# A two-stage convolution and gated projection: the first convolution of all columns on TensorE in small overlapping superblocks, products of two blocks grouped by shape of the array

## The chip, the cores and the metric

The kernel runs on one core of one Trainium2 chip. A core has TensorE (matrix products, in the profile PE, and PEld for its weight loads), VectorE (DVE), ScalarE (ACT), GpSimd (POOL) and SyncE (SP, which here issues DMAs). The metric is the device time of one execution in microseconds; lower is better. Three runs of the kernel before took 463.28, 458.24 and 459.96 us, so the time before is the median, 459.96 us.

## The reference, cut to what matters

```python
# x: (8, 4224, 192), weight: (8, 7), conv_w: (5, 192), w_val and w_out: (192, 192)
w = softmax(weight, axis=-1)                       # one set of 7 taps per head of 24 channels
x_pad = concatenate([zeros(6 rows), x])            # causal
x = einsum('hk,bskhg->bshg', w, x_unf)             # first convolution, per head
gate_pre = 0
for k in range(5):                                 # second convolution, per channel, causal
    gate_pre += conv_w[k] * xp[:, k:k + S, :]
gate = 1 / (1 + exp(-gate_pre))
out = (gate * (x @ w_val)) @ w_out
```

`moe_w_val`, `moe_conv_w` and `moe_w_out` arrive as float64, and their bits are put together to float32 on the chip (`decode`).

## The kernel before, in words

**Layout.** The eight sequences are laid end to end, with zero rows between, in two streams of four sequences each. Channels lie on partitions and time on columns: channels 0 to 127 of the streams side by side in one tile (`x1`, two halves), channels 128 to 191 of both streams stacked in one tile of 128 partitions (`x2`: 64 rows for each stream).

**First convolution.** Columns come in groups (`NJS`, `TOKS`). The first group, 456 columns, is convolved element by element (`conv_first`, L264: ACT, DVE and POOL). All others go through TensorE: a window of 128 rows of x in time (122 new ones and 6 of overlap), 120 channel-and-run columns wide, is the stationary operand; a banded matrix of the softmaxed taps (`band`, one per head, written by SP's DMAs at L170) is the moving one, 122 columns. One window is one float32 matmul, which the trace shows as two instructions. A bank holds up to four windows (`conv_unit`, L309); ACT copies it to a tile `e` (L331). The rows of `e` are then moved to `x1` and `x2` by DMA on SP's queue: for groups 1 and 2 through DRAM (`bounce`, written at L352, gathered at L294 and L298), for the others straight, from five runs of rows to five stretches of columns (`conv_scatter`, L342, issue at L385). The 4 columns of history of a group are copied from the group before by POOL (`conv_edges`, L247).

**Blocks.** Columns are worked in 36 blocks (`STEPS`), mostly of 488. For a block n: `gate_open` (ACT, L407) and four `gate_taps` (DVE, L414) for each of two accumulators in PSUM make the second convolution; `gate_close` is the sigmoid (ACT, L427). `split1` and `split2` write x as a high and a low part of reduced float32 (ACT, then POOL, L435 to L444). The product with `w_val` takes three matmuls for each pair of parts. `product1` (L452) makes channels 0 to 127: for each stream three matmuls with 128 rows (L457 to L459), then three pairs with 64 rows, one in each half of the array's rows (L464). `product2` (L467) makes channels 128 to 191: three matmuls with 128 output columns, half of them zero weights (stream 1), three with 64 output columns (stream 0), both L472, and three with a block-diagonal weight for `x2` (L475). `gated` multiplies with the gate (DVE, L504); the result is split again and goes through the same two products with `w_out`; `project` copies (ACT, L519) and stores. The last block's `w_out` product is made in float32 (`product_whole`, L478).

**Order.** PE, ACT, DVE and POOL run in the order written out at L585 to L609. In turn n: the `w_val` products of block n, taps and split of block n + 1, the `w_out` products of block n - 1, and convolution banks in four places, as many as `due` asks for. 44 convolution units are issued ahead of the loop (L576 and L580). PSUM has eight banks: two for convolution, two and one for the gate's accumulators, three for products.

Of the kernel before, what the change touches and what calls it, by code (L numbers as in the profile page):

```python
# [7 lines left out]
F32 = mybir.dt.float32  # L8
# [4 lines left out]
ALU = mybir.AluOpType  # L13
PSUM = bass.MemoryType.PSUM

# [5 lines left out]
NS = 5  # L21
PADB = S + KW - 1 + KG - 1
SEQS = 4


NP = 456
NJS = [0, 4, 8, 8, 8, 8, 8, 8, 2]
NG = len(NJS)
TOKS = [n * NS * WIN // 2 if n else NP for n in NJS]
STREAM = sum(TOKS)  # L30
EV = [t + t % 2 for t in TOKS]
XC = max(EV) + HALO
RUNM = max(NJS) * WIN

BOUNCED = (1, 2)
XBUFS, EBUFS = 4, 3

LOADS = (0, 1, "x2", "wv", 2, 3, "x3", 4, 5, "wo", 6, 7)


CB = 2
C0 = 28

BLOCKS = {456: (456,), 610: (306, 304), 1220: (408, 406, 406), 2440: (488,) * 5}
MB = 488
STEPS = []
for _g, _t in enumerate(EV):
    _o = 0
    for _n in BLOCKS[_t]:
        STEPS.append((_g, _o, _n))  # L50
        _o += _n

LAST = len(STEPS) - 1


@with_exitstack
def kernel(
# [3 lines left out]
    xc: bass.AP,  # L63
# [15 lines left out]
    dp = ctx.enter_context(tc.tile_pool(name="dp", bufs=1, space=bass.MemoryType.DRAM))  # L79
# [6 lines left out]
    w0 = cp.tile([128, 2, KW], F32, name="w0")  # L86
    nc.sync.dma_start(w0, hw)
    scr = [op.tile([128, 3 * MB], F32, tag="ot", name=f"scr_{i}") for i in range(3)]
# [11 lines left out]

    xpre = gp.tile([128, 2, MB], F32, tag="g1", name="xpre")
    xpre2 = gp.tile([128, MB], F32, tag="g2", name="xpre2")
    NX = NP + KW - 1

    heads = [(g, h) for g in range(1, NG) for h in range(NH)]
    xtiles, xoff, loaded = {}, {}, [0]
    o = 0
    for g, h in heads:
        xoff[g, h] = o
        o += WK * NJS[g] * NS * HC  # L110

    def load_x(i):

        if i != loaded[0] or i == len(heads):
            return
        loaded[0] += 1
        g, h = heads[i]
        n = NJS[g] * NS * HC
        t = xin.tile([WK, max(NJS) * NS * HC], F32, tag="x", name=f"x_{g}_{h}")
        o = xoff[g, h]  # L120
        nc.sync.dma_start(t[:, :n], xw[o : o + WK * n].rearrange("(p f) -> p f", f=n))
        xtiles[g, h] = t

# [3 lines left out]
    with tc.manual_schedule(engines={mybir.EngineType.SP}):  # L127
        nc.sync.dma_start(xpre[:, :, :NX], xc[:, :2, :])
        nc.sync.dma_start(xpre2[:, :NX], xc[:, 2, :])
        load_x(0)  # L130
        load_raw("cw")
        load_x(1)

        one = cp.tile([128, 1], F32, name="one")
        nc.vector.memset(one, 1.0)
        warm = cp.tile([128, 1], F32, name="warm")
        nc.scalar.activation(warm, one, AF.Exp)
        rrow = 2 * WIN + KW

        row = cp.tile([128, 2, rrow], F32, name="row")  # L140
        nc.gpsimd.memset(row, 0.0)

        def wide(t):
            return t[:, :, None].to_broadcast([128, 2, KW])

        mx = cp.tile([128, 2], F32, name="mx")
        nc.vector.tensor_reduce(out=mx, in_=w0, op=ALU.max, axis=mybir.AxisListType.X)
        w1 = cp.tile([128, 2, KW], F32, name="w1")
        nc.vector.tensor_tensor(out=w1, in0=w0, in1=wide(mx), op=ALU.subtract)
        w2 = cp.tile([128, 2, KW], F32, name="w2")  # L150
        nc.scalar.activation(w2, w1, AF.Exp)
        warm2 = cp.tile([128, 1], F32, name="warm2")
        nc.scalar.activation(warm2, w2[:, 0, 0:1], AF.Sigmoid)
        sm = cp.tile([128, 2], F32, name="sm")
        nc.vector.tensor_reduce(out=sm, in_=w2, op=ALU.add, axis=mybir.AxisListType.X)
        sm2 = cp.tile([128, 2], F32, name="sm2")
        nc.vector.tensor_scalar(out=sm2, in0=sm, scalar1=1e-9, scalar2=None, op0=ALU.add)
        rs = cp.tile([128, 2], F32, name="rs")
        nc.vector.reciprocal(rs, sm2)
        taps = row[:, :, WIN - 1 : WIN - 1 + KW]  # L160
        nc.vector.tensor_tensor(out=taps, in0=w2, in1=wide(rs), op=ALU.mult)


        band = cp.tile([WK, NH, WIN], F32, name="band")

        def load_band(h):
            c, p = divmod(h * HC, 128)
            r = row[p : p + 1, c, :]
            src = bass.AP(tensor=r.tensor, offset=r.offset, ap=[list(r.ap[0]), [1, WK], [1, WIN]])
            nc.sync.dma_start(band[:, h, :], src)  # L170

        for k in LOADS:
            if k in raw:
                load_raw(k)
            elif k in ("x2", "x3"):
                load_x(int(k[1]))
            else:
                load_band(k)
# [31 lines left out]
    pr = decode("cw", 2 * KG)  # L210
    put(cwt.rearrange("p a k -> p (a k)"), pr, 0, 128, 0, 2 * KG)

    W11, W21, WZ, W12, W22 = 0, 128, 256, 320, 384
    NW = 512

    class Weight:
        def __init__(self, name):  # L220
            self.name = name
            self.f = cp.tile([128, NW], F32, name=f"{name}f")
            self.h = cp.tile([128, NW], F32R, name=f"{name}h")
            self.l = cp.tile([128, NW], F32R, name=f"{name}l")
            nc.gpsimd.memset(self.f, 0.0)

        def make(self):
# [7 lines left out]
            nc.scalar.copy(self.h, t)  # L235
            nc.vector.tensor_tensor(out=self.l, in0=t, in1=self.h.bitcast(F32), op=ALU.subtract)
# [3 lines left out]
    x1s, x2s = {}, {}  # L240

    def conv_open(g):
        x1 = xp.tile([128, 2 * XC], F32, tag="x1", name=f"x1_{g}")
        x2 = xp.tile([128, XC], F32, tag="x2", name=f"x2_{g}")
        x1s[g], x2s[g] = x1, x2

    def conv_edges(g):  # L247

        x1, x2 = x1s[g], x2s[g]
        x1v = x1.rearrange("p (a t) -> p a t", a=2)  # L250
        if g == 0:
            nc.gpsimd.memset(x1v[:, :, 0:HALO], 0.0)
            nc.gpsimd.memset(x2[:, 0:HALO], 0.0)
        else:
            t = TOKS[g - 1]
            p1 = x1s[g - 1].rearrange("p (a t) -> p a t", a=2)
            nc.gpsimd.tensor_copy(x1v[:, :, 0:HALO], p1[:, :, t : t + HALO])
            nc.gpsimd.tensor_copy(x2[:, 0:HALO], x2s[g - 1][:, t : t + HALO])
        if EV[g] > TOKS[g]:
            t = HALO + TOKS[g]  # L260
            nc.gpsimd.memset(x1v[:, :, t : t + 1], 0.0)
            nc.gpsimd.memset(x2[:, t : t + 1], 0.0)

    def conv_first():  # L264

        conv_open(0)
# [412 lines left out]
```

## Time and profile before

| | us |
|---|---|
| median of three runs | 459.96 |
| the profiled execution, span from first to last instruction | 457.0 |
| TensorE busy | 416.4 |
| VectorE busy | 358.4 |
| ScalarE busy | 327.1 |
| GpSimd busy | 255.1 |

The span lies 3.0 us under the median of the runs. Durations of single instructions on PE, DVE and ACT overlap with the next one's, so a cost per instruction is read from start to start. In a timeline row stand the start, the length, the engine, the line, the operation, the tiles (written<-read), the shape (for a matmul rows*columns of the weights, then the moving operand), the count, and in brackets what the engine waited for. In a table by stretch stand, after the times, the busy time of PE, PEld, DVE, ACT and POOL, the granted clock of TensorE (1.00 is full), the share of the DMA engines and GB/s.

### The profile page before, as it was taken

The numbers are of one execution on the slowest core, as the hardware profiler recorded it, in microseconds if no ns is written. First come the engines' busy times: TensorE is split into PE (matmuls) and PEld (weight loads), VectorE is DVE, ScalarE is ACT, GpSimd is POOL, SyncE is SP. The second block draws the span as 40 slices with busy tenths as digits, with TensorE's granted clock in tenths as the row PEclk, the third lists the DMA queues.
The fourth block names the chain that finished last, engine by engine and source line by source line (L and its number), as shares of the span: only waits on it lengthen the run. The fifth ranks groups of instructions, "written<-read, shape, count | busy, mean of one in ns | idle before, by whom it ended". The sixth has DMA issues, their size and how long they took to land.

```text
span 457.0 us, 7190 instructions
## 1 busy us (share of the span) xinstructions
PE 416.4 (91%) x2371; PEld 321.7 (70%) x2371; DVE 358.4 (78%) x449; ACT 327.1 (72%) x537; POOL 255.1 (56%) x173
## 2 busy tenths in 40 slices
PE   2379659579999999999999999999999999999997
PEld 2268548467777777777777777777777777776773
DVE  5993983346998887888878888788887889999960
ACT  7335356275887777778777777777877788888852
POOL 5900522252776665566655666556665567768750
PEclk9657999969999999999999999999999999999999
DMA  7765855588878987666676766657666553322322
GB/s 199 172 207 186 287 187 195 192 271 199 245 184 255 276 221 225 178 218 207 180 215 183 221 212 174 213 169 224 216 184 200 143 154 101 108 84 89 135 115 99
DMA packets 30989, 85.95 MB, mean 188 GB/s; under 512 B 7272, under 2 KB 14504, under 8 KB 30952
## 3 DMA queue, kind: packets, MB, share of 16 engines
q1 hardware_dynamic: 30952, 85.50, 61.7%
q8 instruction: 18, 0.29, 0.3%
q14 instruction: 19, 0.16, 0.1%
HBM read 33.68 MB, written 31.62 MB: 143 GB/s over the span
## 4 chain that ended last, share of the span: by engine, by line
PE 75%; DMA 18%; ACT 3%; POOL 2%; issue 1%; SPq 0%; ACTq 0%
PE pc L324 15%; DMA bounce<-e 12%; PE pv L472 10%; PE po L472 9%; PE po L464 6%; PE pv L464 6%; PE po L475 5%; PE pv L475 4%; DMA x<-bounce 4%; PE po L457 3%; PE po L459 3%; PE pv L457 3%; PE po L458 3%; PE pv L459 3%; PE pv L458 3%; POOL x L280 2%
## 5 line engine op out<-in xcount | busy, mean ns | idle before, releaser
L414 DVE SCALAR_TENSOR_TENSOR pa<-x,cwt,pa 128x976 f32<-128x976 f32 (+5 forms) x144 | 172.5, 1198 | 18.9 <-ACT pa L407 16.5
L324 PE MATMUL pc<-band,x 128*120 128x122 f32 x864 | 123.4, 290 | 26.6 <-ACT e L331 18.2
L324 PEld LDWEIGHTS pc<-band,x 128*120 128x120 f32 x864 | 113.2, 198 | 45.4 <-ACT e L331 22.2
L436 POOL TENSOR_TENSOR pl<-g,ph 128x976 fp32r<-128x976 f32 (+4 forms) x35 | 78.3, 2236 | 89.8 <-ACT ph L435 85.1
L436 POOL TENSOR_TENSOR xl<-x,xh 128x976 fp32r<-128x976 f32 (+5 forms) x36 | 79.1, 2198 | 82.1 <-ACT xh L435 80.3
L331 ACT COPY e<-pc 120x488 f32<-120x488 f32 (+2 forms) x128 | 63.0, 502 | 74.1 <-PE pc L324 40.6
L504 DVE TENSOR_TENSOR g<-pv,g 128x488 f32<-128x488 f32 (+5 forms) x108 | 66.4, 642 | 52.1 <-ACT pb L407 23.8
L414 DVE SCALAR_TENSOR_TENSOR pb<-x,cwt,pb 128x488 f32<-128x488 f32 (+5 forms) x144 | 102.2, 710 | 3.7
L519 ACT COPY ot<-po 128x488 f32<-128x488 f32 (+5 forms) x108 | 56.0, 553 | 25.1 <-PE po L464 16.2
L444 POOL TENSOR_TENSOR pl<-g,ph 128x488 fp32r<-128x488 f32 (+4 forms) x35 | 42.6, 1217 | 8.0 <-ACT ph L443 8.0
L407 ACT ACTIVATE pa<-x,cwt 128x976 f32<-128x976 f32 (+5 forms) x36 | 37.8, 1051 | 11.7 <-DMA x<-bounce 10.4
L444 POOL TENSOR_TENSOR xl<-x,xh 128x488 fp32r<-128x488 f32 (+5 forms) x36 | 43.1, 1197 | 0.0
L472 PE MATMUL pv<-xh,wvh 128*128 128x488 f32 (+5 forms) x72 | 31.1, 432 | 8.4 <-ACT ot L519 7.6
L427 ACT ACTIVATE g<-pa 128x976 f32<-128x976 f32 (+5 forms) x36 | 34.6, 962 | 5.3 <-DVE pa L414 4.7
L435 ACT CAST xh<-x 128x976 fp32r<-128x976 f32 (+5 forms) x36 | 34.7, 964 | 4.5 <-DMA x<-bounce 2.4
L435 ACT CAST ph<-g 128x976 fp32r<-128x976 f32 (+4 forms) x35 | 34.4, 984 | 0.0
L457 PE MATMUL pv<-xh,wvh 128*128 128x488 f32 (+5 forms) x72 | 29.8, 416 | 2.2 <-DVE g L504 2.2
L472 PE MATMUL po<-ph,woh 128*128 128x488 f32 (+4 forms) x70 | 30.2, 431 | 0.0
L457 PE MATMUL po<-ph,woh 128*128 128x488 f32 (+4 forms) x70 | 29.0, 415 | 0.0
L472 PE MATMUL pv<-xl,wvh 128*128 128x488 f32 (+5 forms) x72 | 27.4, 381 | 0.0
L472 PE MATMUL pv<-xh,wvl 128*128 128x488 f32 (+5 forms) x72 | 27.4, 381 | 0.0
L459 PE MATMUL pv<-xl,wvh 128*128 128x488 f32 (+5 forms) x72 | 27.2, 378 | 0.0
(92 smaller groups left out, 688.9 us busy)
## 6 DMA issues: line engine op xcount, KB each, us to landing
x<-xw SPq DMA_DIRECT2D x48, 480.0 KB
out<-ot SPq DMA_DIRECT2D x30, 732.0 KB
x<-e SPq DMA_DIRECT2D x165, 91.5 KB
bounce<-e SPq DMA_DIRECT2D x8, 457.5 KB
x<-bounce SPq DMA_DIRECT2D x1, 1952.0 KB
x<-xw SPq DMA_DIRECT2D x8, 240.0 KB
bounce<-e SPq DMA_DIRECT2D x8, 228.8 KB
x<-bounce SPq DMA_DIRECT2D x3, 488.0 KB
```

Source lines behind the costliest of these rows:

```text
L324: nc.tensor.matmul(pc[: NS * HC, j * WIN : (j + 1) * WIN], lhsT=xtiles[g, h][:, jj * NS * HC : (jj + 1) * NS * HC], rhs=band[:, h, :], sta ...
L331: nc.scalar.copy(e[: NS * HC, q * hr : (q + 1) * hr], pc[: NS * HC, :hr])
L414: nc.vector.scalar_tensor_tensor(out=acc, in0=views(n, k)[i], scalar=cwt[:, i, k : k + 1], in1=acc, op0=ALU.mult, op1=ALU.add,)
L435: nc.scalar.copy(h, x)
L436: nc.gpsimd.tensor_tensor(out=l, in0=x, in1=h.bitcast(F32), op=ALU.subtract)
L444: nc.gpsimd.tensor_tensor(out=l, in0=x, in1=h.bitcast(F32), op=ALU.subtract)
L457: nc.tensor.matmul(acc, lhsT=w.h[:, r], rhs=h[:, q], start=True, stop=False)
L459: nc.tensor.matmul(acc, lhsT=w.h[:, r], rhs=l[:, q], start=False, stop=False)
L464: nc.tensor.matmul(acc, lhsT=a[p, r], rhs=b[p], start=False, stop=(i == 2))
L472: nc.tensor.matmul(o, lhsT=a[:, r], rhs=b[:, q], start=(q == 1 and i == 0), stop=False)
L504: nc.vector.tensor_tensor(out=v, in0=pvs.pop((n, q)), in1=v, op=ALU.mult)
L519: nc.scalar.copy(ots[n][:, q * m : (q + 1) * m], acc)
```

## The change

All columns are convolved on TensorE. They come in 13 superblocks of n = 1, 2, 4 and then ten times 5 windows for each of five runs, which give 286, 606, 1216 and 1506 columns (the last 1264). Superblocks overlap by the history they need: no columns are copied from the one before, and some windows are made twice (456 windows over all heads in place of 432). The rows of `e` are now in channel-major order and the channels are permuted (`PERM`), so one DMA moves a whole head where it took several: 13 for a superblock. The DRAM tile goes. The band's eight DMAs are issued by ACT.

Blocks are mostly 502 wide; there are again 36. In each, channels 128 to 191 of both streams are made by float32 matmuls of 64 output columns (`columns`), four quarters of the block for two halves of the array's columns, in place of six matmuls on split parts. Products of block n with `w_val` and of block n - 1 with `w_out` are put together by their shape: the diagonal ones, the full ones, the column ones, the row ones. The last block takes the same way as the others. Convolution banks and products share one PSUM pool of five banks. The gate's tiles `g1`, `g2` have two buffers in place of three, `x1`, `x2` three in place of two. The convolution of superblock g is spread over the blocks of superblock g - 2; superblocks 0 and 1 are convolved ahead of the loop. SP's order is written out too.

```diff
-NJS = [0, 4, 8, 8, 8, 8, 8, 8, 2]
+NJS = [1, 2, 4] + [5] * 10
+BLOCKS = {1: (286,), 2: (304, 302), 4: (406, 406, 404), 5: (502, 502, 502)}
+QUADS = ((6, 7, 5, 0), (1, 2, 3, 4))
+PER_LOAD = {1: 4, 2: 2, 4: 1, 5: 1}
+XBUFS, EBUFS = 6, 3
+LAG = 2
...
-    xp = ctx.enter_context(tc.tile_pool(name="xp", bufs=2))
+    xp = ctx.enter_context(tc.tile_pool(name="xp", bufs=3))
...
-    gp = ctx.enter_context(tc.tile_pool(name="gp", bufs=3))
+    gp = ctx.enter_context(tc.tile_pool(name="gp", bufs=2))
...
-    ps_c = ctx.enter_context(tc.tile_pool(name="ps_c", bufs=2, space=PSUM))
...
-    ps_v = ctx.enter_context(tc.tile_pool(name="ps_v", bufs=3, space=PSUM))
+    ps = ctx.enter_context(tc.tile_pool(name="ps", bufs=5, space=PSUM))
...
+    for q in QUADS:
+        for h in q:
...
-            nc.sync.dma_start(band[:, h, :], src)
+            nc.scalar.dma_start(band[:, h, :], src)
...
+        def send(dst, c0, c1, a, b):
+            w = NS * (b - a)
+            dma(dst[:, :w].rearrange("p (s t) -> p s t", s=NS), rows(c0, c1)[:, a:b])
+
+        if h < 5:
+            send(x1[h:120:5], 0, HC, 0, r)
+        else:
+            ends = (0, hf), (r - hf, r)
+            if h == 5:
+                for i, (a, b) in enumerate(ends):
+                    send(x1[120:128, i * second(n) :], 0, 8, a, b)
+            for i, (a, b) in enumerate(ends):
+                if h == 5:
+                    send(x2[64 * i + 48 : 64 * i + 64], 8, HC, a, b)
+                else:
+                    send(x2[64 * i + h - 6 : 64 * i + 48 : 2], 0, HC, a, b)
...
+    def diagonal(what, n):
...
+        r = slice(W22, W22 + 128)
+        for i, (a, b) in enumerate(parts(w, h2, l2)):
+            nc.tensor.matmul(acc, lhsT=a[:, r], rhs=b, start=(i == 0), stop=False)
...
+    def columns(what, n):
...
+        m = STEPS[n][2]
+        acc = banks[what, n, 2]
+        w = w_val if what == "v" else w_out
+        x = views(n)[0] if what == "v" else g1s[n]
+        cuts = [m * i // 4 for i in range(5)]
+        for i in range(4):
+            c = slice(cuts[i], cuts[i + 1])
+            for q, p in enumerate(HALVES):
+                nc.tensor.matmul(
+                    acc[p, c], lhsT=w.f[:, W12 : W12 + 64], rhs=x[:, q, c],
+                    start=False, stop=(i == 3),
+                )
...
+    conv(first_unit[1])
+    w_val.make()
+    load_raw("wo")
+    gate_open(0, 0)
+    gate_open(0, 1)
+    gate_taps(0, 0)
+    gate_taps(0, 1)
+    split(0)
+    gate_close(0, 0)
+    gate_close(0, 1)
+    conv(first_unit[LAG] - done[0])
+    w_out.make()
+    gate_open(1, 0)
+    gate_open(1, 1)
+
+    for n in range(N + 1):
+        todo = max(0, (due[n] if n < N else 0) - done[0])
+        c = [todo // 4 + (i < todo % 4) for i in (3, 0, 2, 1)]
+        diagonal("v", n)
+        gate_taps(n + 1, 0, 1, 3)
+        split(n + 1)
+        diagonal("o", n - 1)
+        main("v", n, 0)
+        conv(c[0])
+        main("v", n, 1)
+        gate_taps(n + 1, 0, 3, KG)
+        columns("v", n)
+        gated(n, 2)
+        gate_close(n + 1, 0)
+        gate_open(n + 2, 0)
+        columns("o", n - 1)
+        split_gated2(n)
+        project(n - 1, 2)
+        rows("v", n)
+        gated(n, 0)
+        gated(n, 1)
+        rows("o", n - 1)
+        split_gated1(n)
+        main("o", n - 1, 0)
+        gate_taps(n + 1, 1)
+        project(n - 1, 0)
+        conv(c[1])
+        main("o", n - 1, 1)
+        conv(c[2])
+        project(n - 1, 1)
+        conv(c[3])
+        gate_close(n + 1, 1)
+        gate_open(n + 2, 1)
```

`main` makes the three full matmuls of one stream (as L457 to L459 before), `rows` the three pairs in the array's two row halves (as L464 before).

More of the change, by code (lines that the diff above doesn't have):

```diff
@@ new lines @@
+    load_x(2)
+    load_raw("cw")
+    load_raw("wv")
+    load_x(4)
+    one = cp.tile([128, 1], F32, name="one")
+    nc.vector.memset(one, 1.0)
+    warm = cp.tile([128, 1], F32, name="warm")
+    nc.scalar.activation(warm, one, AF.Exp)
+    rrow = 2 * WIN + KW
+    row = cp.tile([NH, rrow], F32, name="row")
+    nc.gpsimd.memset(row, 0.0)
+    mx = cp.tile([NH, 1], F32, name="mx")
+    nc.vector.tensor_reduce(out=mx, in_=w0, op=ALU.max, axis=mybir.AxisListType.X)
+    w1 = cp.tile([NH, KW], F32, name="w1")
@@ L247, in conv_edges @@
[L247 to L262, printed above, removed]
@@ L307 @@
[L307 to L323 removed]
+    x1s, x2s, es = {}, {}, {}
@@ L387 @@
-    N = len(STEPS)
-    first = [next(n for n in range(N) if STEPS[n][0] == g) for g in range(NG)] + [N]
-    g1s, g2s, accs, ots, pvs = {}, {}, {}, {}, {}
-    xs, ps = {}, {}
+        a = (ws[0][0] * n + ws[0][1]) * WIN
+        w = len(ws) * WIN
+        nc.scalar.copy(e[:, a : a + w], pc[:M, :w])
+        done = [hi for hi, j in ws if j == n - 1]
+        for hi in done:
+            h = QUADS[q][hi]
+            i, at = home[g, h]
+            if at == len(loads[i][1]) - 1:
+                load_x(i + 1 + XBUFS)
+            scatter(g, h, e[:, hi * n * WIN : (hi + 1) * n * WIN])
@@ L478, in product_whole, with bank @@
-    def product_whole(w, n, q, x1, x2, name):
-        acc = accumulator(n, q, name)
-        f = w.f
-        for i in (q,) if q < 2 else (0, 1):
-            r = HALVES[i]
-            c1, c2, o = (W11, W21, slice(0, 128)) if q < 2 else (W12, W22 + 64 * i, r)
-            k = o.stop - o.start
-            nc.tensor.matmul(acc[o], lhsT=f[:, c1 : c1 + k], rhs=x1[:, i], start=True, stop=False)
-            nc.tensor.matmul(acc[o], lhsT=f[r, c2 : c2 + k], rhs=x2[r], start=False, stop=True)
-        return acc
+    def bank(what, n, q):
+        t = ps.tile([128, 512], F32, tag="p", name=f"{what}_{n}_{q}")[:, : STEPS[n][2]]
+        banks[what, n, q] = t
+        return t
@@ new lines, in operands, with parts, ok @@
+    def operands(what, n):
+        return (w_val, *xs[n, 1], *xs[n, 2]) if what == "v" else (w_out, *pr[n, 1], *pr[n, 2])
+    def parts(w, h, l):
+        return (w.h, h), (w.l, h), (w.h, l)
+    def ok(n):
+        return 0 <= n < N
+    def diagonal(what, n):
+        if not ok(n):
+            return
+        acc = bank(what, n, 2)
+        w, _, _, h2, l2 = operands(what, n)
+        r = slice(W22, W22 + 128)
+        for i, (a, b) in enumerate(parts(w, h2, l2)):
+            nc.tensor.matmul(acc, lhsT=a[:, r], rhs=b, start=(i == 0), stop=False)
@@ new lines, in main, with rows @@
+    def main(what, n, q):
+        if not ok(n):
+            return
+        fresh = (what, n, q) not in banks
+        acc = bank(what, n, q) if fresh else banks[what, n, q]
+        w, h, l, _, _ = operands(what, n)
+        r = slice(W11, W11 + 128)
+        for i, (a, b) in enumerate(parts(w, h, l)):
+            nc.tensor.matmul(
+                acc, lhsT=a[:, r], rhs=b[:, q], start=(fresh and i == 0), stop=(not fresh and i == 2)
+            )
+    def rows(what, n):
+        if not ok(n):
+            return
+        fresh = (what, n, 0) not in banks
+        two = [bank(what, n, q) if fresh else banks[what, n, q] for q in range(2)]
+        w, _, _, h2, l2 = operands(what, n)
+        r = slice(W21, W21 + 128)
+        for i, (a, b) in enumerate(parts(w, h2, l2)):
+            for acc, p in zip(two, HALVES):
+                nc.tensor.matmul(
+                    acc, lhsT=a[p, r], rhs=b[p], start=(fresh and i == 0), stop=(not fresh and i == 2)
+                )
@@ new lines, in conv @@
+            if done[0] < len(units):
+                conv_unit(done[0])
+                done[0] += 1
+    due = []
+    for n in range(N):
+        total = first_unit[LAG]
+        for g in range(LAG, NG):
+            a, b = at[first[g - LAG]], at[first[g - LAG + 1]]
+            share = min(1.0, max(0.0, (at[n + 1] - a) / (b - a)))
+            total += round(share * (first_unit[g + 1] - first_unit[g]))
+        due.append(total)
+    pr_cw = decode("cw", 2 * KG)
+    put(cwt.rearrange("p a k -> p (a k)"), pr_cw, 0, 128, 0, 2 * KG)
```

501 lines of the change are left out of this document (171 added, 330 removed).

## The prediction

> **What bounds the kernel now.** I read the page's busy shares first, then busy time by stretch, then the chain of waits, then TensorE's own timeline.
>
> ```profile
> PE 416.4 (91%) x2371; PEld 321.7 (70%) x2371; DVE 358.4 (78%) x449; ACT 327.1 (72%) x537; POOL 255.1 (56%) x173
> ```
> ```profile
> 0.00:57.00 57.00, 33.31 (x177) 28.86 (x177) 43.85 (x71) 27.25 (x52) 23.97 (x26) 0.79 0.70 210
> 57.00:114.00 57.00, 43.41 (x260) 36.59 (x258) 30.73 (x39) 31.23 (x55) 16.93 (x11) 0.88 0.67 209
> 172.50:229.80 57.30, 57.30 (x341) 44.17 (x340) 47.17 (x56) 45.48 (x72) 35.11 (x22) 1.00 0.67 201
> 387.30:425.00 37.70, 37.70 (x192) 27.08 (x191) 36.99 (x45) 32.07 (x56) 28.20 (x19) 1.00 0.30 106
> ```
> After the times in each row come PE, PEld, DVE, ACT, POOL, clock, DMA share, GB/s. There are two regimes. Up to 114 us TensorE works 76.7 of 114 us, partly at a lowered clock; after that it never rests. The third row is five blocks of 488 columns (11.46 us each) with convolution beside them, the fourth four blocks with almost none (9.43 each; DVE 36.99 of 37.70, so VectorE is nearly full too).
>
> ```profile
> 19.13 8.38 DMA bounce<-e
> ...
> 62.01 13.93 DMA bounce<-e
> ...
> 92.72 10.24 DMA x<-bounce
> ...
> 170.18 1.34 PE po L472 x6
> ...
> 227.45 1.33 PE po L472 x6
> ```
> The chain says what the first regime waits for: columns written to DRAM and gathered back. In the second it is TensorE alone; the same product returns after five blocks, 57.27 us.
>
> ```profile
> 251.13 0.38 PE L472 MATMUL po<-pl,woh 128*128 128x488 f32 x1
> 251.35 0.39 PE L472 MATMUL po<-ph,woh 128*64 128x488 f32 x1
> ...
> 252.68 1.00 PE L324 MATMUL pc<-band,x 128*120 128x122 f32 x8
> 253.44 0.47 PE L457 MATMUL po<-ph,woh 128*128 128x488 f32 x1
> 253.74 0.39 PE L458 MATMUL po<-ph,wol 128*128 128x488 f32 x1
> ...
> 254.63 0.39 PE L459 MATMUL po<-pl,woh 128*128 128x488 f32 x1
> 254.95 0.48 PE L464 MATMUL po<-ph,woh 64*128 64x488 f32 x2
> 255.27 0.39 PE L464 MATMUL po<-ph,wol 64*128 64x488 f32 x2
> 255.49 0.39 PE L464 MATMUL po<-pl,woh 64*128 64x488 f32 x2
> 255.81 0.49 PE L472 MATMUL pv<-xh,wvh 128*128 128x488 f32 x1
> 256.13 0.39 PE L472 MATMUL pv<-xh,wvl 128*128 128x488 f32 x1
> ```
> Durations overlap, so I count from start to start. A reduced-float32 matmul of 488 columns costs a slot of 0.222 us, whether it fills 128 or 64 output columns (251.13 to 251.35). A pair in the two 64-row halves costs one slot, not two: the halves run at once. Around such pairs four gaps are 0.31 to 0.32 instead of 0.22: an excursion to row halves costs 0.39 us extra. Eight convolution instructions (four windows, two passes each) and the next slot fill 252.68 to 253.74: 0.105 us an instruction, nothing for the change of kind.
>
> Check: a block has 2 x 18 slots (8.0), two excursions (0.78) and 3.2 convolution banks of 0.84 (2.69): 11.47, against 11.46 measured. The same columns at 502 a block are 11.79.
>
> **The change on TensorE, per block of 502.** A slot becomes 0.222 x 502/488 = 0.228. Diagonal, main and row products of both matrices are (3 + 6 + 3) x 2 = 24 slots, 5.47. Grouping both matrices' row products leaves one excursion, 0.39. A superblock has 40 windows in three blocks: 13.33 x 2 x 0.105 = 2.80. What replaces 12 slots (2.74) are 16 float32 matmuls of 125 columns, 32 passes, in two column halves of the array. No row shows two column halves at work together. The nearest rows are the last block's float32 products and the convolution's weight loads:
>
> ```profile
> 448.17 0.72 PE L486 MATMUL po<-g,wof 128*64 128x304 f32 x2
> 448.83 0.72 PE L487 MATMUL po<-g,wof 64*64 64x304 f32 x2
> ...
> 450.79 0.78 PE L486 MATMUL po<-g,wof 128*128 128x304 f32 x2
> 451.50 0.78 PE L487 MATMUL po<-g,wof 64*128 64x304 f32 x2
> ```
> ```profile
> 252.45 1.03 PEld L324 LDWEIGHTS pc<-band,x 128*120 128x120 f32 x8
> ```
> Two passes of 304 columns with 64 weight columns take 0.66, with 128 take 0.71: 64 weight columns cost about 0.05 where nothing covers them. A pass by the convolution's rate is 0.105 x 304/122 = 0.26, so 0.66 - 0.05 - 0.52 leaves a switch of about 0.09. In the convolution eight loads lie inside the eight matmuls. A pass of 125.5 columns is then 0.105 x 125.5/122 = 0.108. Lowest: a half's second pass overlaps the other half's first, 17 steps, 1.84 us. Taking turns: 32 x 0.108 = 3.46. Highest, with a load and a switch at every matmul as in the last block: 16 x (0.216 + 0.14) = 5.7. I take 1.84, as the row halves, the nearest packed rows, overlap fully, plus 0.15 for one more switch of shape. Sum: 5.47 + 0.39 + 2.80 + 1.84 + 0.15 = 10.65.
>
> The Trainium skill ("TensorE: Matmul & The Clock Gate", The mechanism) says that weight loads overlap running matmuls only where their row groups differ. Column halves share all rows, so by it each of the 17 steps would be 0.158 and the block 11.5 (an estimate); the trace disagrees in the convolution, where loads on the same rows are hidden. The same page reports 2.38x for three column tiles; no run here shows it.
>
> **Who else must keep up.** From the third window, five blocks, scaled to 502: DVE 47.17/5 = 9.43, so 9.70; ACT 9.10, so 9.36 (at most: copies of convolution banks fall from 128 to 114); POOL 7.2. All fit under 10.65. New waits: the sigmoid's target has two buffers for three, so a block's gate closing on ACT waits until the column products two blocks back have been read; behind it on ACT queue the next gate opening, a split and a projection copy. In my layout of a block VectorE finishes the taps at 4.4 and the column products end at 4.8, a 0.4 us wait, after which ACT still has over 1 us spare. Five shared banks serve nine uses a block; the copies come back within 2 us of use. I add 0.25 for hand-overs: **10.9 a block**. The last six blocks have no convolution: TensorE needs 7.8, VectorE 9.70; I take 9.9, close to the fourth window.
>
> **Queues and the start.**
>
> ```profile
> L385 SPq DMA_DIRECT2D x<-e x288: 513/733/1968, 95.7 to 421.6; - x144
> ...
> L170 SPq DMA_DIRECT2D band<-row x8: 476/604/1346, 3.9 to 12.8; - x8
> ```
> ```profile
> 8.18 4.01 PE L324 MATMUL pc<-band,x 128*120 128x122 f32 x20 [8.18 <-DMA band<-row]
> ```
> ```profile
> L414 DVE SCALAR_TENSOR_TENSOR pa<-x,cwt,pa 128x608 f32<-128x608 f32 x4 | 3.4, 852 | 0.1
> ...
> L414 DVE SCALAR_TENSOR_TENSOR pb<-x,cwt,pb 128x304 f32<-128x304 f32 x4 | 2.2, 538 | 0.1
> ```
> Scatters become 13 for each of 13 superblocks, 169 for 288 (at 0.73 us of SP each, 123 for 211 us), and the bounce writes and gathers go; in steady state this is hidden, 8 issues a block. At the start it is the chain. The eight band issues move from SP to ACT: 8 x 0.6 = 4.8 us of ACT, free of them SP sends windows, but ACT's first bank copy is queued behind them. First matmul still at about 8, superblock 0's banks copied at 11.5 and 13. Then 13 scatters (9.5) and four loads on SP, and some 2.5 us of landing (the first band took 4.3 from issue to matmul, beside big loads): 25. Gate 0 of 286 columns: opening, taps of 3.4 and 2.2 us at most, closing: 32. Superblock 1's copies stand behind that closing on ACT: four, then 13 scatters (9.5) and landing: the loop opens at **44**. The elementwise convolution of the first 456 columns goes; it stood beside the waits and gives nothing by itself. Decoding the weights stays on VectorE under the same waits; without that cover it would stand in front of gate 0.
>
> Short blocks: block 0 with 8 banks, 10; block 1 9.5, and 5 waiting for superblock 2; block 2 9.5; three of 406 columns by the same slots 9.4: **62**. Then 24 x 10.9 = **262**; five of 9.9 and one of 260 columns, 5.5: **55**. Last products, now through the split on POOL and not float32, with copy and store: **6**, as long as today's tail. Span 44 + 62 + 262 + 55 + 6 = **429**, against 457.0. The median of the runs shown is 459.96, 3.0 above this profile's span; hence 432, say **433 us**.
>
> **Rivals.**
> - *Column halves take turns* (ends on the other side). For it: nothing here shows columns overlapping, and the two passes of one matmul stand next to each other in the queue. Against: row halves overlap. The block becomes 10.65 + 1.62 = 12.3, with hand-overs some 12.4: 24 x 1.5 more, and 6 in the short blocks; the last six stay under VectorE. 433 + 42 = **475**. It decides once the 32 passes take over about 2.9 us, where the loss eats start and steady gain together.
> - *Loads exposed in column halves* (the row-group mechanism above): 17 x 0.05 = 0.9 a block on 24 blocks, 4 on the others: **459**, no change. Against it: the convolution's hidden loads.
> - *The start does not shorten*: ACT serves gate 0, superblock 1's copies and gate 1 strictly in turn, and a 13-scatter burst stands before each gate. If each of three bursts costs 5 us more, **448**.
> - *Every matmul pays load and switch*, as in the last block: 5.7 - 1.84 = 3.9 a block more, but 2 to 3 in short and last ones: **545**.
>
> **How the numbers follow.** Forecast 0.55; late start or slow hand-overs 0.17; exposed loads 0.12; taking turns 0.11; all exposed 0.05. Within 1% (455 to 465) is about what a measurement here cannot tell from none. Faster: 0.55 + 0.17 and a quarter of the exposed-loads case, 0.75; same 0.10; slower 0.15. The forecast's own range is 418 to 446 (0.4 us a block either way, 5 us of start). For 8 in 10 it must take in the late start and the exposed loads: 415 to 462, which leaves out the two serial cases.
>
> **What would show it.** Starts of the column passes: 32 within 1.8 us confirm, 3.4 refute. One 0.39 excursion a block. No DRAM tile in the chain; the loop's first products near 44 us. In 110 to 370 us TensorE busy all through and VectorE near 90%. If TensorE has holes there ended by ACT or VectorE, the gate-closing wait or the five banks are dearer than 0.25 us. Wrong would also be a start whose scatters land after 50 us.

## The result, and the profile after

| | before | after |
|---|---|---|
| median, us (four runs each) | 460.36 | 438.11 |
| range of the runs, us | 458.24 to 463.28 | 437.04 to 439.16 |
| profiled execution, span, us | 457.0 | 434.6 |

The ratio of after to before is 0.949, with a 95% interval of 0.942 to 0.955. The kernel became 5% faster. The forecast was 433 us with a range of 415 to 462, and its mechanism in the steady part was right; the start did not go as it said, as the views show.

First the busy shares on the page of the changed kernel, and its chain of waits by engine:

```profile
PE 378.8 (87%) x3144; PEld 321.0 (74%) x3144; DVE 346.4 (80%) x443; ACT 319.9 (74%) x517; POOL 236.2 (54%) x151
...
PE 76%; SPq 5%; DMA 5%; DVE 4%; ACT 4%; ACTq 3%; issue 2%; DVEq 0%
```

TensorE's busy time fell from 416.4 to 378.8 us, by 37.6. Its idle time rose, from 457.0 - 416.4 = 40.6 to 434.6 - 378.8 = 55.8 us, by 15.2. The difference is the 22.4 us gained. No DRAM tile is left in the chain, but ScalarE's DMA issues (ACTq) and SP's (SPq) stand in it now.

Busy time by stretch places this. The bounds are the points at which ScalarE can start on gate 1 (55.60), and the first products on TensorE of block 1 (65.24), block 6 (122.38, the first of 502 columns) and block 30 (376.31, the first without convolution beside it). The columns are those of the prediction's table. Gate 0, gate 1 and gate 2 stand from here on for the first gate opening on the columns of superblock 0, 1 and 2; a scatter is one of the 13 DMAs that move a superblock's rows of `e` to `x1` and `x2`.

```profile
0.00:55.60 55.60, 19.14 (x95) 15.99 (x95) 18.73 (x55) 10.24 (x19) 2.83 (x9) 0.78 0.50 106
55.60:65.24 9.64, 6.94 (x48) 6.95 (x49) 8.54 (x14) 7.99 (x15) 4.41 (x4) 0.66 0.40 112
65.24:122.38 57.14, 47.86 (x473) 44.55 (x472) 39.24 (x54) 40.10 (x75) 26.48 (x20) 0.91 0.81 227
122.38:376.31 253.93, 253.93 (x2131) 214.47 (x2130) 233.57 (x265) 220.48 (x345) 166.02 (x97) 1.00 0.77 220
376.31:434.60 58.29, 50.94 (x406) 38.99 (x404) 46.27 (x58) 41.06 (x66) 36.44 (x23) 0.97 0.31 116
```

In the fourth row TensorE is busy all the time and VectorE 92% of it: 24 blocks take 253.93 us, 10.58 each. A block of as many columns took 11.79 before, scaled from the 11.46 of 488 columns. All idle time of TensorE but 7.4 us lies ahead of 122 us: 48.4 us, where before had 37.3 ahead of 114. So the change is a gain in the steady part, and the start gives some of it back.

The start, in ScalarE's timeline:

```profile
4.23 13.85 ACTq L195 DMA_DIRECT2D band<-row  x7
18.12 0.56 ACT L287 COPY e<-pc 120x488 f32<-120x488 f32 x1 [13.86 <-DMA band<-row]
...
33.18 0.74 ACT L342 ACTIVATE pa<-x,cwt 128x572 f32<-128x572 f32 x1 [9.55 <-DMA x<-e]
...
39.46 0.41 ACT L362 ACTIVATE g<-pb 128x286 f32<-128x286 f32 x1 [1.44 <-DVE pb L349]
39.76 1.97 ACT L287 COPY e<-pc 120x488 f32<-120x488 f32 x4
...
55.61 0.77 ACT L342 ACTIVATE pa<-x,cwt 128x608 f32<-128x608 f32 x1 [10.47 <-DMA x<-e]
...
80.22 0.94 ACT L342 ACTIVATE pa<-x,cwt 128x812 f32<-128x812 f32 x1 [10.27 <-DMA x<-e]
```

One engine's row is read downwards as a chain: seven band DMAs take 13.85 us to issue, so the first bank is copied only at 18.12; its scatters open gate 0 at 33.18; superblock 1's four banks are copied behind gate 0's closing, at 39.76; their scatters open gate 1 at 55.61. At 80.22 ScalarE has stood another 10.27 us for superblock 2, in block 1's turn. SP's rows between the copies and gate 1 show thirteen scatters, with four window loads between them:

```profile
40.35 1.60 SPq L308 DMA_DIRECT2D x<-e  x2
42.05 0.46 SPq L136 DMA_DIRECT2D x<-xw  x1
42.56 4.39 SPq L308 DMA_DIRECT2D x<-e  x6
...
52.23 0.78 SPq L308 DMA_DIRECT2D x<-e  x1
```

And the steady part, in TensorE's timeline: the column products of both matrices, and the first row product behind them:

```profile
230.99 0.40 PE L415 MATMUL v<-xl,wvh 128*128 128x502 f32 x1
231.32 1.08 PE L443 MATMUL v<-x,wvf 128*64 128x125 f32 x16
232.24 1.03 PE L443 MATMUL o<-g,wof 128*64 128x125 f32 x16
233.20 0.49 PE L428 MATMUL v<-xh,wvh 64*128 64x502 f32 x2
```

The 32 passes in column halves take from 231.32 to 233.20, 1.88 us: 16 steps of 0.105, in each of which both halves run a pass, and 0.20 around them. Another 0.10 lies ahead of the first pass (230.99 to 231.32, for a slot of 0.228).

### The profile page after: what moved, and what is told of

Read it like the earlier page. It is cut to its first block, busy times and chain, and to the rows that moved or that the text cites. A ratio compares the mean times of both kernels' runs of the same rounds, so it can differ in the third digit from the quotient of the medians.

```text
span 434.6 us, 8458 instructions
## 1 busy us (share of the span) xinstructions
PE 378.8 (87%) x3144; PEld 321.0 (74%) x3144; DVE 346.4 (80%) x443; ACT 319.9 (74%) x517; POOL 236.2 (54%) x151
## 3 DMA queue, kind: packets, MB, share of 16 engines
q10 hardware_dynamic: 1152, 0.50, 2.1%
## 4 chain that ended last, share of the span: by engine, by line
PE 76%; SPq 5%; DMA 5%; DVE 4%; ACT 4%; ACTq 3%; issue 2%; DVEq 0%
PE pc L278 20%; PE o L415 12%; PE v L415 10%; PE v L443 7%; PE o L443 6%; PE v L428 6%; PE o L428 5%; PE v L405 5%; PE o L405 5%; DMA x<-e 4%; SPq L308 4%; ACTq L195 3%; DVE pa L349 2%; DVE pb L349 1%; SPq L136 1%
## 5 line engine op out<-in xcount | busy, mean ns | idle before, releaser
L349 DVE SCALAR_TENSOR_TENSOR pa<-x,cwt,pa 128x1004 f32<-128x1004 f32 (+6 forms) x144 | 172.9, 1201 | 32.6 <-ACT pa L342 28.8
L371 POOL TENSOR_TENSOR xl<-x,xh 128x1004 fp32r<-128x1004 f32 (+6 forms) x36 | 73.1, 2031 | 126.2 <-ACT xh L370 119.9
L349 DVE SCALAR_TENSOR_TENSOR pb<-x,cwt,pb 128x502 f32<-128x502 f32 (+6 forms) x144 | 102.2, 710 | 3.8
L458 DVE TENSOR_TENSOR g<-v,g 128x502 f32<-128x502 f32 (+6 forms) x108 | 65.9, 642 | 27.0 <-PE v L428 17.9
L371 POOL TENSOR_TENSOR pl<-g,ph 128x1004 fp32r<-128x1004 f32 (+6 forms) x36 | 79.3, 2203 | 8.2 <-ACT ph L370 6.2
L287 ACT COPY e<-pc 120x488 f32<-120x488 f32 x114 | 62.2, 581 | 19.7 <-DMA band<-row 13.9
L379 POOL TENSOR_TENSOR pl<-g,ph 128x502 fp32r<-128x502 f32 (+6 forms) x36 | 43.3, 1204 | 57.9 <-ACT ph L378 57.9
L362 ACT ACTIVATE g<-pa 128x1004 f32<-128x1004 f32 (+6 forms) x36 | 34.4, 957 | 49.3 <-PE o L443 23.0
L342 ACT ACTIVATE pa<-x,cwt 128x1004 f32<-128x1004 f32 (+6 forms) x36 | 37.8, 1050 | 31.4 <-DMA x<-e 30.3
L474 ACT COPY ot<-o 128x502 f32<-128x502 f32 (+6 forms) x108 | 59.4, 555 | 1.2 <-PE o L415 0.7
L379 POOL TENSOR_TENSOR xl<-x,xh 128x502 fp32r<-128x502 f32 (+6 forms) x36 | 41.2, 1146 | 0.0
```

The lines of the kernel that those rows point to most:

```text
L287: nc.scalar.copy(e[:, a : a + w], pc[:M, :w])
L349: nc.vector.scalar_tensor_tensor(out=acc, in0=views(n, k)[i], scalar=cwt[:, i, k : k + 1], in1=acc, op0=ALU.mult, op1=ALU.add,)
L371: nc.gpsimd.tensor_tensor(out=l, in0=x, in1=h.bitcast(F32), op=ALU.subtract)
L379: nc.gpsimd.tensor_tensor(out=l, in0=x, in1=h.bitcast(F32), op=ALU.subtract)
L458: nc.vector.tensor_tensor(out=v, in0=banks.pop(("v", n, q)), in1=v, op=ALU.mult)
L474: nc.scalar.copy(ots[n][:, q * m : (q + 1) * m], banks.pop(("o", n, q)))
```

## The experiments

The theory that the runs had to test: the gain is TensorE's, from column halves that run together and from putting shapes together; the start lost because the band's loads got slower, because superblock 1 was convolved behind gate 0, and because superblock 2's transfers are late. Times of one kernel spread over 2 to 5 us, so where a run has one time, the verdict rests on places in its trace. In the job of the first four runs the kernel before took 463.7 us, in that of the second four 463.3.

### The band's source rows spread over the partitions

```diff
...
-            r = row[h : h + 1, :]
+            r = row[16 * h : 16 * h + 1, :]
...
```

The weights are repeated 16 times, so that head h's taps are made in partition 16h. In the kernel before they lay in partitions 24h modulo 128; the change had moved them to 0 to 7.

> Edit: the eight rows that the band is read from stand on partitions 0, 16, 32 ... 112 in place of 0 to 7; ACT still issues. Theory A (the band is late because its eight sources lie on neighbouring partitions): the band's packets fall from 127 ns towards the 28 ns of the kernel before, ACT's first bank copy comes from 18.1 to about 12 us, and the span falls by 5 to 6 us to about 429. Theory B (the band is late because ACT's issues wait in turn for earlier DMAs, whatever the source): the issues still take 14 us, first copy at 17 to 18.5, span 433 to 436.

It took 433.75 us. Its ScalarE timeline:

```profile
4.56 8.23 ACTq L195 DMA_DIRECT2D band<-row  x7
12.83 0.57 ACT L287 COPY e<-pc 120x488 f32<-120x488 f32 x1 [8.29 <-DMA band<-row]
...
50.42 0.77 ACT L342 ACTIVATE pa<-x,cwt 128x608 f32<-128x608 f32 x1 [10.56 <-DMA x<-e]
```

Issuing falls from 13.85 to 8.23 us, the first copy comes 5.3 us earlier and gate 1 opens 5.2 us earlier. The gain is 3.1 us by the end of the span, less than the 5 to 6 expected: ScalarE waits 11.28 us for superblock 2 in place of 10.27, so that gate 2 opens 4.0 us earlier (76.19), and the last microsecond is within the spread of single runs. The packets show where the time at the start went. ScalarE's queue carries nothing but the band; its row in the page's list of queues, of the changed kernel and of this one:

```profile
q10 hardware_dynamic: 1152, 0.50, 2.1%
```
```profile
q10 hardware_dynamic: 1152, 0.50, 1.4%
```

A packet takes 0.021 x 16 x 434.6 / 1152 = 0.127 us on average with neighbouring source partitions and 0.084 with spread ones; the medians of the 488-byte packets are 132 and 27 ns. The median overstates it: 62% of them take over 100 ns with neighbouring partitions, and still 37% with spread ones.

### The band issued by SP, from the same partitions

```diff
-            nc.scalar.dma_start(band[:, h, :], src)
+            nc.sync.dma_start(band[:, h, :], src)
```

> Edit: the eight band DMAs are issued by SP again, from the same neighbouring partitions. Theory A (sources on neighbouring partitions): the packets stay slow, above 100 ns, and the first bank copy stays at 16 to 19 us. Theory B (it is ACT as the issuer, or its queue): the packets fall towards 28 ns, the first copy comes at about 11 to 13 us, and the span falls by 5 to 7 us.

It took 438.65 us. SP's timeline:

```profile
3.99 14.41 SPq L195 DMA_DIRECT2D band<-row  x8
```

SP needs 14.41 us for the eight, the packets' median is 131 ns, the first copy comes at 17.11 and gate 1 opens at 55.98. So the move from SP to ScalarE, which the prediction had priced, is not what made the start late; the move of the source rows, which it had not seen, is.

### The column halves one after the other

```diff
-        for i in range(4):
-            c = slice(cuts[i], cuts[i + 1])
-            for q, p in enumerate(HALVES):
+        for q, p in enumerate(HALVES):
+            for i in range(4):
+                c = slice(cuts[i], cuts[i + 1])
```

> Edit: the eight float32 column matmuls are issued half by half (four quarters of stream 0, then four of stream 1) in place of alternating. Theory A (the alternating halves of the array run at once): their 16 passes for each product take 1.65 to 1.75 us in place of 0.92, a block with convolution goes from 10.63 to about 12.2 us, and the span from 434.6 to 475 to 485. Theory B (what overlaps are the two passes of one matmul, not the halves): no change, 432 to 438.

It took 454.4 us, between the two theories' numbers. TensorE's timeline around one block's column products:

```profile
238.98 1.25 PE L443 MATMUL v<-x,wvf 128*64 128x125 f32 x13
239.96 0.32 PE L443 MATMUL o<-g,wof 128*64 128x125 f32 x1
240.06 0.27 PE L443 MATMUL v<-x,wvf 128*64 128x125 f32 x1
...
240.34 1.19 PE L443 MATMUL o<-g,wof 128*64 128x126 f32 x13
241.46 0.50 PE L428 MATMUL v<-xh,wvh 64*128 64x502 f32 x2
```

The 32 passes take 2.48 us in place of 1.88. Passes of the next product start among the last of this one: the other half's work is begun ahead of passes queued earlier, but only over a short distance (the first four passes of the first half start alone, 0.108 apart). So the halves overlap by themselves, and the order in which they are issued decides how much.

### Quarters not cut

```diff
-        cuts = [m * i // 4 for i in range(5)]
-        for i in range(4):
+        cuts = [0, m]
+        for i in range(1):
...
-                    start=False, stop=(i == 3),
+                    start=False, stop=(i == 0),
```

> Edit: the float32 column matmuls are not cut into quarters (one for each stream and product, 502 columns wide). Theory A (equal passes of the two halves start together): 8 passes in 4 steps of 0.42 us, 1.7 us for both products as before; span 432 to 438. Theory B (a half's second pass overlaps the other half's first pass, as the prediction had it): 5 steps of 0.42, 2.1 us, a block 0.3 to 0.4 us longer, span 441 to 446.

It took 436.59 us, the same as the changed kernel:

```profile
231.85 1.06 PE L443 MATMUL v<-x,wvf 128*64 128x502 f32 x4
232.75 1.01 PE L443 MATMUL o<-g,wof 128*64 128x502 f32 x4
233.69 0.49 PE L428 MATMUL v<-xh,wvh 64*128 64x502 f32 x2
```

Both column products take 1.84 us from start to start. Equal passes of the two halves start together (6 ns apart); the quarters give nothing. The prediction's picture, in which a half's second pass runs beside the other half's first and one step is left over, was wrong, though its size was right.

### One more change of shape

```diff
+        rows("v", n)
         columns("o", n - 1)
         split_gated2(n)
         project(n - 1, 2)
-        rows("v", n)
```

> Edit: the row-half products of w_val are issued before the column products of w_out instead of behind them, so that a block has more changes of the array's shape (columns, rows, columns, rows for columns, rows). Theory: each excursion costs what it cost before (0.35 to 0.39 us), so a block becomes 0.3 to 0.5 us longer, 11.0 to 11.1 for 10.63, and the span 441 to 446. Rival: a change between column halves and row halves is nothing by itself, the block stays at 10.6 to 10.7 and the span within 3 us of 434.6.

It took 445.99 us. By stretch, three blocks of its steady part and all 24 that have convolution beside them, and then three blocks of the changed kernel:

```profile
176.29:209.07 32.78, 32.78 (x268) 26.35 (x266) 29.45 (x34) 27.61 (x45) 20.81 (x12) 1.00 0.79 222
124.01:385.76 261.75, 261.75 (x2132) 210.78 (x2130) 235.84 (x266) 220.49 (x345) 166.04 (x97) 1.00 0.75 213
```
```profile
172.16:204.06 31.90, 31.90 (x268) 26.82 (x268) 29.25 (x34) 27.60 (x44) 20.77 (x12) 1.00 0.80 227
```

10.93 us a block for 10.63: 0.29 us for the same 268 matmuls in another order. Over the 24 blocks it is 261.75 for 253.93 us, 0.33 a block, at the lower end of the theory's 0.3 to 0.5. The span is 443.7, 9.1 us more. So changes between column and row halves are paid for.

### The kernel before with column quarters, nothing put together

```diff
-        for q, (o, r) in ((1, (acc, slice(WZ, WZ + 128))), (0, (acc[:64], slice(W12, W12 + 64)))):
-            for i, (a, b) in enumerate(((w.h, h), (w.l, h), (w.h, l))):
-                nc.tensor.matmul(o, lhsT=a[:, r], rhs=b[:, q], start=(q == 1 and i == 0), stop=False)
...
+        for i in range(4):
+            c = slice(cuts[i], cuts[i + 1])
+            for q, p in enumerate(HALVES):
+                nc.tensor.matmul(
+                    acc[p, c], lhsT=w.f[:, W12 : W12 + 64], rhs=x[:, q, c],
+                    start=False, stop=(i == 3),
+                )
```

> The kernel before, with channels 128 to 191 of the first 128 input channels made by float32 matmuls of 64 output columns in the two column halves (as in the changed kernel) instead of six split matmuls; products of two blocks are not put together. Theory: per product six slots of 0.222 (1.33 us) become eight steps of about 0.105 (0.82 to 0.92 with a switch into and out of the column halves, 0.1 to 0.3 in all): TensorE gains 0.2 to 0.4 us a product, 0.4 to 0.8 us a block of 488 columns (11.46 before), and the time falls to 438 to 450. Rival: every product pays an excursion of 0.39 as row halves did, and the gain is at most 0.1 us a product: 455 to 464.

It took 458.15 us: the theory's 438 to 450 fell, the rival's range held, though the gain of 0.15 us a product, read below, lies between the two. Five blocks by stretch, and TensorE's timeline around one column product:

```profile
189.70:245.49 55.79, 55.79 (x441) 41.94 (x440) 47.54 (x56) 45.45 (x73) 35.03 (x22) 1.00 0.71 206
```
```profile
254.24 0.39 PE L472 MATMUL po<-pl,woh 128*128 128x488 f32 x1
254.56 1.06 PE L479 MATMUL po<-g,wof 128*64 128x122 f32 x16
255.54 1.10 PE L324 MATMUL pc<-band,x 128*120 128x122 f32 x8
...
256.71 0.38 PE L458 MATMUL po<-ph,wol 128*128 128x488 f32 x1
```

A block takes 11.16 us for 11.46, a gain of 0.30. The eight steps are cheap (8 x 0.102 = 0.82), but the excursion into column halves is not: 0.10 ahead of the first pass (254.24 to 254.56 is 0.32 for a slot of 0.222), 0.16 in the passes' own stretch (0.98), and 0.11 behind (255.54 to 256.71 is 1.17, where eight convolution instructions and a slot took 1.06 before). That is 0.37, about the 0.39 of an excursion to row halves. So of the 1.16 us that the changed kernel gains on a block of 502 columns (11.79 to 10.63), the column products alone would bring 0.31, and 0.85 is left for putting the shapes of two matrices together. The second number is a difference, of which the run before showed a part by itself. The prices come near it: put together, a block has one row excursion (0.39) and one column excursion (0.37) fewer, 0.76. Putting together without the column products was not run.

### The kernel before without its DRAM tile

```diff
-BOUNCED = (1, 2)
+BOUNCED = ()
```

> The kernel before, with groups 1 and 2 scattered straight into their tiles like the others instead of through the DRAM tile; nothing else is changed. Theory (from the changed kernel, whose start is as long without a DRAM tile): the bounce by itself costs nearly nothing, because the straight scatters of the same groups (36 issues each at about 0.73 us, 26 us of SP) take as long; the time stays at 455 to 468. Rival: the bounce was what held the start of the kernel before; without it the time falls to 440 to 450.

It took 477.1 us, 14 more than the kernel before beside it, outside both theories. The chain's shares between 38 and 127 us:

```profile
by line: SPq L385 40.2%; DMA x<-e 14.5%; PE pc L324 9.2%; issue 5.1%; ACT pa L407 3.4%; ACT e L331 2.9%; PE pv L472 2.7%; SPq L121 2.5%; PE pv L475 2.3%; PE po L472 1.6%; ACT ot L519 1.6%; ACT g L427 1.5%; ACT pb L407 1.4%; PE pv L457 1.4%;
```

SP's issues of scatters take the place of the bounce: this kernel issues 384 in all for 288, 48 for each of the two groups, where the expectation had counted 36. With so many the DRAM tile was the better way, so taking it away is no gain by itself; in the changed kernel 13 scatters for a superblock stand in its place.

### Superblock 1 convolved ahead of gate 0

```diff
-    load_x(4)
+    load_x(6)
...
-    conv(first_unit[1])
+    conv(first_unit[LAG])
...
-    conv(first_unit[LAG] - done[0])
```

> Edit: the convolution of superblock 1 is issued before gate 0 instead of behind it, and six window loads are sent at once instead of four. Theory: the loop opens late because superblock 1's four bank copies stand behind gate 0 on ScalarE (gate 0 closes at 39.8 us in the changed kernel) and its 13 scatters behind those. Then superblock 1's scatters follow superblock 0's at once on SP, and the loop's first products move from 55.6 us to about 45; if the block-1 wait for superblock 2 shrinks with it, the span falls from 434.6 to 423 to 427. Rival: the wait at block 1 (10 us, superblock 2's scatters landing beside loads at over 200 GB/s) only grows by what the loop gains, and the span stays at 431 to 436.

It took 435.85 us, the rival's time, but by another wait than the rival's. ScalarE's timeline:

```profile
53.50 0.51 ACT L248 CAST woh<-wof 128x384 fp32r<-128x384 f32 x1 [14.36 <-DVE wof L224]
53.92 0.77 ACT L342 ACTIVATE pa<-x,cwt 128x608 f32<-128x608 f32 x1
```

Gate 1's opening no longer waits for a scatter. It stands behind the cast of `w_out`, whose load is now issued behind 26 scatters on SP, at 43.37. A wait was removed, and the next in the same queue took its place.

### The same, with that load ahead of superblock 1's scatters

```diff
...
     conv(first_unit[1])
+    load_raw("wo")
+    conv(first_unit[LAG] - done[0])
     w_val.make()
-    load_raw("wo")
...
```

> As e5_early_conv, and the load of w_out's raw bits is put between the scatters of superblock 0 and those of superblock 1 on SP. Theory: in e5_early_conv superblock 1 had landed by about 45 us, but gate 1's opening stood on ScalarE behind w_out's cast (53.50 us), which waited for that load, issued behind all 26 scatters. With the load ahead of them the loop's first products move from 53.9 us (e5) to 44 to 48, the span to 423 to 430 if the wait for superblock 2 does not eat it. Rival: superblock 1's scatters themselves land only at 52 to 54 us and the opening stays there, span 432 to 436.

It took 427.04 us:

```profile
45.91 0.77 ACT L342 ACTIVATE pa<-x,cwt 128x608 f32<-128x608 f32 x1 [1.85 <-DMA x<-e]
...
70.01 0.94 ACT L342 ACTIVATE pa<-x,cwt 128x812 f32<-128x812 f32 x1 [9.07 <-DMA x<-e]
```

Gate 1 opens at 45.91 for 55.61, 9.7 us earlier, gate 2 10.2 earlier, and the span is 9.6 shorter: what the start gains here reaches the end whole.

### Both corrections of the start

The edits of the run before and of the first experiment, together.

> e11_early_conv_wo and e1_band_spread together (the band's source rows spread over the partitions, superblock 1 convolved before gate 0, w_out's load ahead of its scatters). Theory: the two gains lie one behind the other in the chain to the loop's opening (5 us and 8 to 11 us), so the loop opens at 39 to 43 us for 55.6, and the span is 418 to 425, some 10 to 15 us under the changed kernel. Rival: the wait at block 1 for superblock 2's scatters takes most of it back, span 427 to 432.

It took 423.10 us (422.57 to 424.52, four runs), 0.916 of the kernel before, interval 0.913 to 0.918. Gate 1 opens at 42.55, gate 2 at 67.35, the span is 422.4, 12.2 us under the changed kernel's. The two gains do not quite add up: gate 1 opens 13.1 us earlier, for 9.7 and 5.2. The wait for superblock 2 is 9.5 us and did not take the gain back.

### Half of superblock 2 convolved ahead of the loop

```diff
+    conv(4)
     w_out.make()
     gate_open(1, 0)
```

> e12_starts, and the first four of superblock 2's eight convolution units are issued ahead of the loop, while gate 1 waits for superblock 1. Theory: the 10 us wait at block 1 is the time from superblock 2's convolution inside block 0's turn to the landing of its scatters; with half of them issued earlier it falls by 3 to 7 us, span 413 to 420. Rival: the wait is for the transfers themselves (7.34 us of landing beside window loads at over 200 GB/s), and issuing earlier only moves it: within 2 us of e12_starts.

It took 418.89 us (418.28 to 419.65, four runs), 0.906, interval 0.904 to 0.908.

```profile
40.66 0.77 ACT L342 ACTIVATE pa<-x,cwt 128x608 f32<-128x608 f32 x1 [1.68 <-DMA x<-e]
...
61.78 0.94 ACT L342 ACTIVATE pa<-x,cwt 128x812 f32<-128x812 f32 x1 [9.33 <-DMA x<-e]
```

From gate 1 to gate 2 it is 21.1 us, for 24.8 in the run before; ScalarE, which has less to copy in between, still waits 9.33. Of the 5.6 us by which gate 2 opens earlier these are 3.7; the other 1.9 lie ahead of gate 1, on whose way the edit takes nothing out, and stay unexplained. The span is 417.6.

### Superblock 3's window loads behind superblock 2's scatters

The loads that went out between superblock 2's scatters on SP are held back to the last of these.

```diff
-            if at == len(loads[i][1]) - 1:
+            if at == len(loads[i][1]) - 1 and (g != LAG or i < first_load[LAG] + 2):
                 load_x(i + 1 + XBUFS)
             scatter(g, h, e[:, hi * n * WIN : (hi + 1) * n * WIN])
+        if u + 1 == first_unit[LAG + 1]:
+            load_x(first_load[LAG + 1] + XBUFS)
```

> As e13_starts_sb2, and the six window loads of superblock 3 (300 KB each), which went out between superblock 2's scatters on SP, are issued behind the last of these. Theory: the 9.3 us wait at block 1 that is left is for the transfers: from 40 to 58 us the DMA engines move 200 GB/s, of which those loads are 1.8 MB, about 9 us; without them superblock 2 has landed 4 to 9 us earlier, gate 2 opens at 53 to 58 us for 61.8, and the span is 409 to 414 if superblock 3's windows are not late. Rival 1: the scatters' own issue on SP (13 x 0.8 us) and TensorE's convolution set the wait, gate 2 opens at 60 to 62, span 416 to 419. Rival 2: superblock 3's convolution now waits for its windows and TensorE stands in blocks 1 to 3, span 419 or more.

It took 417.53 us (417.00 to 418.78, four runs), 0.909 of the kernel before in its job, interval 0.904 to 0.915. The intervals of this run and the one before overlap, so no gain is shown. TensorE's and ScalarE's timelines:

```profile
56.21 1.95 PE L279 MATMUL pc<-band,x 128*120 128x122 f32 x8 [7.41 <-DMA x<-xw]
```
```profile
61.20 0.67 ACT L365 ACTIVATE g<-pa 128x604 f32<-128x604 f32 x1 [2.43 <-PE o L446]
61.90 0.94 ACT L345 ACTIVATE pa<-x,cwt 128x812 f32<-128x812 f32 x1
```

The theory's 53 to 58 us for gate 2 fell. ScalarE no longer waits for superblock 2's scatters at gate 2, which have landed when it comes there; but TensorE, and ScalarE behind it, wait 7.41 us for superblock 3's windows, and gate 2 opens at 61.90, no earlier than the 61.78 before. That is rival 2's wait, though at no cost beyond the one that it replaced. In this stretch both the scatters and the windows are needed within a few microseconds of each other, and holding one back exchanges one wait for the other. How much of it is SP's issuing and how much the transfers stays open; smaller loads weren't tried. The last two versions are the fastest of the study, at 0.906 and 0.909 of the kernel before, where the change alone gave 0.949.

## Why the prediction was right, and where it was not

The forecast's layout of the span beside the measured one, by the table of stretches:

| | forecast | measured | difference |
|---|---|---|---|
| gate 1 can open, loop runs | 44 | 55.6 | +11.6 |
| blocks 0 to 5 | 62 | 66.8 | +4.8 |
| 24 blocks with convolution | 262 | 253.9 | -8.1 |
| last blocks and tail | 61 | 58.3 | -2.7 |
| span | 429 | 434.6 | +5.6 |

**Steady part: right, and its safety margin was not needed.** The sum of 10.65 us met 10.63 in the three blocks from 172.16 (10.58 over all 24, in the first of which the products with `w_out` have 404 columns). Slots of 0.228, convolution at 0.105 an instruction and both column products at 1.88 with 0.10 ahead of them (forecast 1.84 + 0.15) came as worked out from rows of the kernel before. The 0.25 for hand-overs was not paid: TensorE was busy for 253.93 of 253.93 us. The wait that it was for did come, off the path; the list of groups on the page shows ScalarE idle 49.3 us ahead of gate closings, 23.0 of them ended by the column products:

```profile
L362 ACT ACTIVATE g<-pa 128x1004 f32<-128x1004 f32 (+6 forms) x36 | 34.4, 957 | 49.3 <-PE o L443 23.0
```

**Column halves.** Of the rivals, taking turns, exposed loads and a load and switch at every matmul fell. (The 545 us of the last doesn't follow from its own terms: 3.9 on 24 blocks and 2 to 3 on the other twelve give 551 to 563.) The Trainium skill ("TensorE: Matmul & The Clock Gate", The mechanism) has the rule that weight loads overlap matmuls only where row groups differ, though it also names a background weight buffer as a way to load ahead; by the rule a step was estimated at 0.158 us. Both halves use all rows, and a step took 0.105, so the measurement decides against the rule here, as the convolution's row did in the kernel before; no run shows whether such a buffer is the reason. How far the halves take turns is a matter of the order issued: issued half by half, they took 0.60 us a block more in the third experiment.

**The start: the step that failed.** "Superblock 0's banks copied at 11.5", from "8 x 0.6 = 4.8 us of ACT", was wrong by 6.6 us (18.12). The diff had moved the rows that those DMAs read to neighbouring partitions, which the prediction did not mention; with the rows spread again the first copy came at 12.83, so 5.3 of the 6.6 us go to that. There too the copy stood behind the issues, which ended at 12.79, so the other 1.3 us are in their price. The 0.6 was a median; the same row of the kernel before gave 476 to 1346 ns as the lengths of the eight, and in SP's timeline they take 6.1 us together, with other loads between them:

```profile
3.91 1.23 SPq L170 DMA_DIRECT2D band<-row  x2
...
7.14 1.12 SPq L170 DMA_DIRECT2D band<-row  x2
...
8.94 1.73 SPq L170 DMA_DIRECT2D band<-row  x2
...
11.45 1.99 SPq L170 DMA_DIRECT2D band<-row  x2
```

On ScalarE, with spread rows, they took 8.8 (0.54 for the first and 8.23 for the other seven). From the copy to gate 0 it was 15.1 us for 13.5, and from gate 0's closing to gate 1 15.7 for 12, where four window loads went out between the scatters and the forecast had none. The prediction named "scatters land after 50 us" as a sign of being wrong, and that sign came. The time held because the steady part was 8 us better than the forecast; that the two errors nearly cancelled is luck.

**Block 1's wait for superblock 2** was in the sum with 5 us and was 10.3. Half of its convolution issued earlier shortened the way from gate 1 to gate 2 by 3.7 us; taking the loads out of the scatters' way only changed who waits.

**The last blocks** are VectorE's, as said: it is busy 18.61 of 19.00 us.

```profile
395.00:414.00 19.00, 17.52 (x126) 12.90 (x126) 18.61 (x22) 14.60 (x23) 13.52 (x9) 0.95 0.21 82
```

**The rival "the start does not shorten"** (448, from three bursts of 5 us each) was right about the start: 11.6 and 4.8 are 16.4 us there. Only part of that is its three bursts, though: 6.6 us lie ahead of the first of them, with the band. Its total was not reached because the steady part and the end were 10.8 us shorter than the forecast.

## What to carry to other kernels

On a saturated TensorE, count slots and changes of the array's shape, each from start to start in the trace: here one excursion more or less was worth 0.3 to 0.4 us, and putting the shapes of two products together was worth more than making one product cheaper. At the start, follow each queue and each engine's order from the first DMA to the first gate, and ask of each wait that is removed what stands next behind it: convolving superblock 1 early gained almost nothing until the load of `w_out` was moved too, and then 9.7 us. Price a burst of DMA issues by their lengths together in the timeline, not by their number times a median, and ask whether the change moves what they read.

## What the runs showed of the hardware that was not expected

- The band's DMAs, which each read one partition, are slower when those partitions are neighbours: a packet takes 0.127 us on average from partitions 0 to 7 and 0.084 from partitions 16 apart (median for 488 bytes 132 and 27 ns). From partitions 0 to 7 it is the same whether ScalarE or SP issues them (132 and 131 ns). The cause inside the DMA path stays open.
- Two column halves of the array run float32 passes fully together, each with its own weight load hidden: 32 passes of 125 columns, with 32 loads, in 1.88 us. Cutting the operand into quarters makes no difference to it (1.84 us uncut).
- A half's pass can start ahead of passes of the other half that were queued before it, over a distance of about four passes (issued half by half, the 32 take 2.48 us).
- A lone excursion to column halves costs as much as one to row halves, 0.37 us for 0.39, though 64 output columns without a second half cost nothing extra (a slot of 0.22 us either way in the kernel before).
